# Running sums for the attention bias, copied 32 times into DRAM in the first phase and read back row by row

## The chip, the cores and the metric

The kernel runs on one core of a Trainium2 chip. The metric is the device time of one execution in microseconds (us). The core has a matrix engine (PE, with its weight loads PEld), three engines for elementwise work (DVE, ACT, POOL), and a queue for transfers on SP; ACT can issue transfers too. DMA means a transfer between the chip's memory (DRAM) and the on-chip memory of 128 partitions (SBUF). PE writes into eight banks.

## The reference, cut to what matters

```python
# q, k, v: [4 batches, 8 heads, 576 positions, 64], s: [4, 8, 576]
cum   = np.cumsum(np.maximum(s, 0.0), axis=-1)
bias  = -(cum[:, :, :, None] - cum[:, :, None, :])
scores = q @ k.T / 8 + np.minimum(bias, 0.0)      # causal: later keys at -1e9
attn  = softmax(scores)                            # normalised with + 1e-9
x = (attn @ v) as 2304 tokens of 512
x = ((x @ w_a) * (x @ w_b)) @ w_out                # inner width 1536
h = x @ w_in                                       # inner width 2048
out = (max(h, 0) + alpha * min(h, 0)) @ w_out2
```

Each of the 32 rows of running sums (batch and head) has 576 values. The bias of a query is the row minus the query's own value, so a tile of scores with 128 queries in its partitions needs the whole row in each of its partitions.

## The kernel before, in words

The 2304 tokens go through the two feed-forward layers in four blocks of 512, 512, 512 and 768. A batch has 576 positions: the first 512 queries of a batch (`u` = 0) and the last 64 (`u` = 1) are handled apart. `first_attention` (L887) computes the first 512 queries of batch 0 alone, ahead of everything. Then each block's feed-forward matmuls (`ffn`, L1248 to L1250 and L1886 to L1888) are mixed with the attention steps for the next block, which `attention(blk)` lists.

Each product is computed from values split into a high and a low part (`xh`, `xl`, `wh`, `wl`), three matmuls each. Weights come as 64-bit numbers (`raw`), are decoded by ACT (`top`, L1029) and DVE (`w`, L292), stored to DRAM as 32-bit numbers (`w_d`), and read from there by later blocks.

The running sums: `s` is loaded into `s_sb` (32 partitions), DVE clips and scales it (L385) and sums along it (L386) into `cum`. L387 writes the 32 rows to DRAM (`cum_d`). For batches 0 and 1 (`SUMS_PE` = 2) and `u` = 0 the bias is added on PE from `cums` and `rows` (L557), which are made from `cum` right afterwards (L390 to L404). All other tiles use `load_sums` (L518): it reads a row of `cum_d` into the 128 partitions of `cb`, and `biases` (L606 on DVE, L610 on ACT) subtracts the query's value `cumq`. For `u` = 0 and batches 2 and 3 a load serves one head: one DMA reads 512 values of one row 128 times (16 loads). For `u` = 1 it serves two heads with 64 queries each: two DMAs read 576 values of a row 64 times each (32 DMAs).

The program fixes the order on each engine. It is made by a planner (`Order`) that runs through estimated times: each operation has a cost, and engines take the operation that can start first. `dma` (L315) counts 480 ns on SP, then 700 ns, then a time by its bytes and a landing time, and a chain with several DMAs plans each behind the landing of the one before. Steps of attention are put between feed-forward matmuls when the planner sees their inputs ready (`possible`). Each engine and each queue works in its program order: an instruction that waits holds up those behind it.

In the first microseconds ACT copies 16 small pieces of the unit matrix (`one_of`, L372), then runs one `Exp` on one column (L890). SP issues the load of `s` (L891), loads of `kq` for the first heads, the store of `cum_d` (L387), and more loads of `kq` and `v`. Weights are requested at `i == FROM_WEIGHTS` (2) in the loop of `first_attention`, five loads of `raw` of 512 KB.

Of the kernel before, what the change touches and what calls it, by code (L numbers as in the profile page):

```python
# [9 lines left out]
F32 = mybir.dt.float32  # L10
# [11 lines left out]
P = 128  # L22
# [26 lines left out]
def f32(ap):  # L49
    return ap.bitcast(F32)  # L50
# [16 lines left out]


FASTER, BEFORE, BEHIND, EARLY = 1.06, 6, 4, 4


SEVEN, PLAIN_1, PLAIN_2 = 3, 3, 4
# [139 lines left out]
def attention_two_moe_kernel(  # L212
# [10 lines left out]
    nc = tc.nc  # L223
    B, S, _ = v.shape
    H = kq_a.shape[1]
# [6 lines left out]
    QA = 4 * P  # L232
    QB = S - QA
# [5 lines left out]
    dram = ctx.enter_context(tc.tile_pool(name="dram", bufs=1, space=DRAM))  # L239
# [6 lines left out]
    raw = inner.enter_context(tc.tile_pool(name="raw", bufs=1))  # L246
    work = inner.enter_context(tc.tile_pool(name="work", bufs=1))
# [67 lines left out]
    def dma(o, i):  # L315
        yield {"sp": 480}, 700
        nc.sync.dma_start(o, i)
        yield {"dma": prod(o.shape) / (180 if o.dtype == U16 else 90)}, run.landing
# [14 lines left out]
    ident = const.tile([P, P], F32, name="ident")  # L333
# [20 lines left out]


    BH = B * H
    cum = raw.tile([BH, S + QB], F32, name="cum", tag="pb")
    cum_d = dram.tile([BH, S], F32, name="cum_d")
    cumq = const.tile([P, NR, BH], F32, name="cumq")


# [3 lines left out]
    NE = SUMS_PE * H  # L365
# [18 lines left out]
    def running_sums(s_sb):  # L384
        nc.vector.tensor_scalar(s_sb, s_sb, 0.0, 8.0, op0=ALU.max, op1=ALU.mult)  # L385
        nc.vector.tensor_tensor_scan(cum[:, 0:S], s_sb, s_sb, 0.0, op0=ALU.add, op1=ALU.max)  # L386
        nc.sync.dma_start(cum_d, cum[:, 0:S])  # L387
        nc.vector.tensor_copy(cum[:, S:S + QB], cum[:, QA:S])
        for i in range(0, P, D):
            nc.scalar.activation(cums[i:i + NE], cum[0:NE, 0:QA], AF.Copy)  # L390
            if i == 0:
                nc.vector.tensor_tensor(
                    cums[BH:BH + NE], cum[0:NE, 0:QA], f32(cums[0:NE]), op=ALU.subtract
                )
            else:
                nc.vector.tensor_copy(cums[i + BH:i + BH + NE], f32(cums[BH:BH + NE]))
        bases = acc[3][:, 0:4 * NE].rearrange("p (r b) -> p r b", b=NE)
        for r in range(4):
            nc.tensor.matmul(
                bases[:, r, :], cum[:, r * P:r * P + 1].to_broadcast([BH, P]), ident[:BH, 0:NE],  # L400
                start=True, stop=True,
            )
        nc.vector.scalar_tensor_tensor(
            rows, bases, less[:, 0:1], one_of, op0=ALU.mult, op1=ALU.add  # L404
        )
        sums = acc[2][:, 0:NR * BH].rearrange("p (r b) -> p r b", b=BH)
        for r in range(NR):
            nc.tensor.transpose(sums[:, r, :], cum[:, r * P:(r + 1) * P], ident[:BH, :BH])
        nc.vector.tensor_scalar(cumq[:, 0:4, :], sums[:, 0:4, :], -1.0, None, op0=ALU.mult)
        for j in range(2):  # L410
            own = slice(j * QB, (j + 1) * QB)
            nc.vector.tensor_scalar(
                cumq[own, 4, 0:BH // 2], sums[own, 4, j:BH:2], -1.0, None, op0=ALU.mult
            )
# [22 lines left out]
    def slot():  # L437

        ring.append(ring.pop(0))
        if ring[-1] in reader:  # L440
            run.need(reader[ring[-1]])
        return ring[-1]
# [53 lines left out]
    def load_kq(b, hp, u):  # L496

        got = []

        def chain():  # L500
            if not u and b >= STACK:
                halves = [run.spawn(stack(b, 2 * hp + j, got), run.t) for j in range(2)]
                yield halves[0]
                yield halves[1]
                return
            yield of_kq
            kq = raw.tile([P, 2 * QA], F32, name="kq", tag="kq", bufs=KQ)
            got.append(kq)
            if u:
                yield from dma(kq[:, 0:S + P], kq_b[b, hp])  # L510
            else:
                for j in range(2):
                    own = slice(j * D, (j + 1) * D)
                    yield from dma(kq[own], kq_a[b, 2 * hp + j, own])

        kq_t[b, hp, u] = got, run.spawn(chain())

    def load_sums(b, h, u):  # L518

        got = []  # L520

        def chain():
            yield of_c1 if u else of_c0
            nk = S if u else QA
            cb = raw.tile([P, nk], F32, name=f"cb{u}", tag=f"cb{u}", bufs=2 if u else CB)
            got.append(cb)
            n = P // (u + 1)
            for j in range(u + 1):
                bh = b * H + (u + 1) * h + j
                yield from dma(  # L530
                    cb[j * n:(j + 1) * n], cum_d[bh:bh + 1, 0:nk].to_broadcast([n, nk])
                )

        cb_t[b, h, u] = got, run.spawn(chain())

    def q_k(b, hp, r, dst):

        got, ready = kq_t[b, hp, 0]
        run.need(ready)
        n = P * (r + 1)  # L540
        if b >= STACK:
            for d, (qs, kh, kl) in zip(dst, got):
                for i, k in enumerate((kh, kl)):
                    nc.tensor.matmul(  # L544
                        d, qs[:, r * P:n], k[:, 0:n], start=i == 0, stop=i == 1
                    )
            run.pe(4 * (n / 2.4 + 13))
            if r == 3:
                kq_t.pop((b, hp, 0))
                for s in (of_kl, of_w32, of_w32, of_stack) * 2:  # L550
                    run.give(s)
            return
        own = [slice(j * D, (j + 1) * D) for j in range(2)]
        if b < SUMS_PE:
            for j, o in enumerate(own):
                bh = b * H + 2 * hp + j
                nc.tensor.matmul(  # L557
                    dst[j], rows[o, r, bh:bh + 1].to_broadcast([D, P]), cums[o, 0:n], start=True,
                    stop=False,
                )  # L560
            run.pe(n / 2.4)
        for j, o in enumerate(own):
            nc.tensor.matmul(  # L563
                dst[j], got[0][o, QA + r * P:QA + n], got[0][o, 0:n], start=b >= SUMS_PE, stop=True
            )
        run.pe(4 * n / 2.4)
        if r == 3:
            kq_t.pop((b, hp, 0))
            run.give(of_kq)
# [63 lines left out]
    def both(b, hp, rs):  # L633
        for j in range(2):
            biases(b, 2 * hp + j, rs)
# [90 lines left out]
    def s23(b, hp, r):  # L726
        at = [slot(), slot()]
        dst = [banks[i][:, 0:P * (r + 1)] for i in at]
        q_k(b, hp, r, dst)
        for j, d in enumerate(dst):  # L730
            soften(b, 2 * hp + j, (r,), [d], at[j])
# [152 lines left out]

    HP = H // 2

    def first_attention():  # L887
        nonlocal ahead
        s_sb = work.tile([BH, S], F32, name="s_sb", tag="z4")
        nc.scalar.activation(alpha_sb[:, 0:1], ident[:, 0:1], AF.Exp)  # L890
        nc.sync.dma_start(s_sb, s)  # L891
        for i in range(2):
            load_kq(0, i, 0)
        run.now = 2000.0
        run.pump()
        running_sums(s_sb)
        run.now = 5000.0
        for rs in ((0, 1), (2,)):
            both(0, 0, rs)
        for i in range(HP + 2):  # L900
            if i + 2 < HP:
                load_kq(0, i + 2, 0)
            if i < HP:
                load_v(0, i, 0)
                both(0, i, (3,))
                s01(0, i)
                if i + 1 < HP:
                    both(0, i + 1, (0, 1))
            if 0 <= i - 2:
                av(0, i - 2, 0)  # L910
            if i < HP:
                s23(0, i, 2)
                if i + 1 < HP:
                    both(0, i + 1, (2,))
                s23(0, i, 3)
            if i == FROM_WEIGHTS:
                nc.sync.dma_start(alpha_sb, alpha)
                ahead = AHEAD
                prefetch()
            if i == FROM_LEAD:  # L920
                for f, args in plan[0][0]:
                    f(*args)
            if 0 <= i - 1 < HP:
                for c in range(3):
                    for j in range(2):
                        turn(0, 2 * (i - 1) + j, c)
            if i >= FROM_STEPS:
                for f, args in plan[0][1][:STEPS]:
                    f(*args)
                del plan[0][1][:STEPS]  # L930
# [978 lines left out]
    for blk in range(NB):  # L1909
# [11 lines left out]
        if 1 <= blk < NB - 1:  # L1921
            n = max(0, blk * S + QA - blocks[blk + 1][0])
# [72 lines left out]
```

## Time and profile before

| what | value |
|---|---|
| time of the runs, median (lowest to highest) | 985.03 us (984.52 to 985.04), 3 runs |
| span of the profiled execution, first to last instruction | 982.3 us |
| what lies around the span, against the median | 2.7 us |
| PE busy | 963.1 us (98%) |
| DVE, ACT, POOL busy | 748.5, 558.7, 223.7 us |
| moved by DMA | 196.78 MB, mean 200 GB/s |

The profiled execution has no time of its own besides its span, so the difference of 2.7 us is taken as what an execution needs before its first and after its last instruction. PE is busy nearly all the time, so what matters is the few microseconds in which it is not.

### The profile page before, as it was taken

The numbers are of one execution on the slowest core, as the hardware profiler recorded it, in microseconds if no ns is written. First come the engines' busy times: TensorE is split into PE (matmuls) and PEld (weight loads), VectorE is DVE, ScalarE is ACT, GpSimd is POOL, SyncE is SP. The second block draws the span as 40 slices with busy tenths as digits, with TensorE's granted clock in tenths as the row PEclk, the third lists the DMA queues.
The fourth block names the chain that finished last, engine by engine and source line by source line (L and its number), as shares of the span: only waits on it lengthen the run. The fifth ranks groups of instructions, "written<-read, shape, count | busy, mean of one in ns | idle before, by whom it ended". The sixth has DMA issues, their size and how long they took to land.

```text
span 982.3 us, 15862 instructions
## 1 busy us (share of the span) xinstructions
PE 963.1 (98%) x5235; PEld 810.3 (82%) x5235; DVE 748.5 (76%) x1743; ACT 558.7 (57%) x1173; POOL 223.7 (23%) x290
## 2 busy tenths in 40 slices
PE   6989999999999999999999999999999999999998
PEld 5557787778888878888888888888899999999997
DVE  7777886986878788888478868666497888787782
ACT  6856675775855555665455547544552333476453
POOL 2131110431124234563135434522100000000000
PEclk9999999999999999999999999999999999999999
DMA  7589999899788979688388785855402212112101
GB/s 181 185 262 320 347 332 322 293 323 329 245 271 259 304 245 312 194 257 293 112 270 260 218 264 194 251 172 183 165 22 94 78 66 87 43 47 82 61 5 65
DMA packets 140083, 196.78 MB, mean 200 GB/s; under 512 B 35744, under 2 KB 79776, under 8 KB 140000
## 3 DMA queue, kind: packets, MB, share of 16 engines
q1 hardware_dynamic: 130208, 177.93, 58.0%
q10 hardware_dynamic: 9792, 17.83, 4.9%
q8 instruction: 41, 0.67, 0.3%
q14 instruction: 42, 0.34, 0.1%
HBM read 152.13 MB, written 43.59 MB: 199 GB/s over the span
## 4 chain that ended last, share of the span: by engine, by line
PE 84%; DMA 8%; DVE 5%; issue 1%; ACT 1%; SPq 0%; POOL 0%; ACTq 0%; DVEq 0%
PE bank L1248 18%; PE bank L1249 18%; PE bank L1250 18%; PE bank L1886 5%; PE bank L1888 4%; PE bank L1887 4%; DMA cb<-cum_d 3%; PE bank L1735 2%; PE bank L1734 2%; PE bank L1736 2%; PE bank L801 2%; DMA raw<-in_w_dram 2%; PE bank L563 2%; PE bank L544 1%; PE bank L741 1%
## 5 line engine op out<-in xcount | busy, mean ns | idle before, releaser
L1248 PE MATMUL bank<-xh,wh 128*128 128x512 f32 (+1 forms) x620 | 237.9, 384 | 2.0 <-DVE g L292 2.0
L1250 PE MATMUL bank<-xh,wl 128*128 128x512 f32 (+1 forms) x620 | 234.0, 377 | 0.0
L1249 PE MATMUL bank<-xl,wh 128*128 128x512 f32 (+1 forms) x620 | 234.0, 377 | 0.0
L284 ACT ACTIVATE wh<-raw 128x512 fp32r<-128x512 f32 (+1 forms) x198 | 115.1, 592 | 84.4 <-PE bank L1249 35.0
L1248 PEld LDWEIGHTS bank<-xh,wh 128*128 128x128 f32 x620 | 116.4, 188 | 26.1 <-issue 4.6
L1250 PEld LDWEIGHTS bank<-xh,wl 128*128 128x128 f32 x620 | 116.4, 188 | 19.3
L1249 PEld LDWEIGHTS bank<-xl,wh 128*128 128x128 f32 x620 | 116.4, 188 | 18.6
L301 POOL TENSOR_TENSOR wl<-raw,wh 128x512 fp32r<-128x512 f32 x69 | 91.5, 1329 | 110.9 <-ACT wh L284 71.1
L301 DVE TENSOR_TENSOR wl<-raw,wh 128x512 fp32r<-128x512 f32 (+1 forms) x135 | 84.6, 640 | 33.7 <-ACT wh L284 27.8
L276 ACT ACTIVATE z<-z,mn 128x512 f32<-128x512 f32 (+4 forms) x144 | 82.8, 577 | 47.3 <-DVE mn L292 45.9
L1248 PE MATMUL bank<-gh,wh 128*128 128x512 f32 (+1 forms) x240 | 89.5, 373 | 0.0
L1249 PE MATMUL bank<-gl,wh 128*128 128x512 f32 (+1 forms) x240 | 88.7, 370 | 0.4 <-DVE gl L301 0.2
L1250 PE MATMUL bank<-gh,wl 128*128 128x512 f32 (+1 forms) x240 | 88.5, 369 | 0.0
L284 ACT ACTIVATE gh<-g 128x512 fp32r<-128x512 f32 x84 | 52.8, 629 | 43.5 <-DVE g L292 40.1
L1886 PE MATMUL bank<-wh,gh 128*128 128x512 f32 x192 | 76.4, 398 | 0.0
L1029 ACT ACTIVATE top<-raw 128x512 f16<-128x512 bf16 x90 | 68.5, 784 | 12.3 <-DMA raw<-in_w_dram 10.9
L1888 PE MATMUL bank<-wh,gl 128*128 128x512 f32 x192 | 74.8, 389 | 0.0
L1887 PE MATMUL bank<-wl,gh 128*128 128x512 f32 x192 | 74.8, 389 | 0.0
L301 DVE TENSOR_TENSOR gl<-g,gh 128x512 fp32r<-128x512 f32 x69 | 51.6, 748 | 18.8 <-ACT gh L284 18.0
L292 DVE STREAM_TRANSPOSE zt<-z 128x384 f32<-128x384 f32 (+2 forms) x88 | 55.7, 648 | 2.4 <-DMA zd<-zt 1.4
L616 POOL TENSOR_SCALAR_AFFINE_SELECT z<-z 64x64 f32<-64x64 f32 (+2 forms) x80 | 34.0, 432 | 97.3 <-DVE z L606 63.7
L311 DVE TENSOR_SCALAR z<-z,sm 128x512 f32<-128x512 f32 (+4 forms) x100 | 55.0, 573 | 1.3
(151 smaller groups left out, 1918.1 us busy)
## 6 DMA issues: line engine op xcount, KB each, us to landing
raw<-w_d SPq DMA_DIRECT2D x91, 512.0 KB, 4.3
raw<-in_w_dram SPq DMA_DIRECT2D x90, 512.0 KB, 5.6
w_d<-w ACTq DMA_DIRECT2D x46, 256.0 KB, 5.0
zd<-zt SPq DMA_DIRECT2D x48, 192.0 KB, 5.0
pt<-zd SPq DMA_DIRECT2D x48, 192.0 KB, 4.9
kq<-in_kq_a_dram SPq DMA_DIRECT2D x16, 512.0 KB, 5.7
vb<-in_v_dram SPq DMA_DIRECT2D x112, 64.0 KB, 4.4
zd<-zt SPq DMA_DIRECT2D x24, 256.0 KB, 4.0
```

The costliest lines, as they stand in the source:

```text
L276: nc.scalar.activation(o, i, func, **k)
L284: nc.scalar.activation(o, i, AF.Copy, scale=by)
L292: f(*args, **k)
L301: (nc.gpsimd if eng == "pool" else nc.vector).tensor_tensor(o, i0, i1, op=ALU.subtract)
L311: (nc.gpsimd if eng == "pool" else nc.vector).tensor_scalar(o, i, s0, s1, op0=ALU.mult, op1=ALU.mult)
L1029: nc.scalar.activation(top.bitcast(F16).rearrange("p (n t) -> p n t", t=2)[:, :, 1], r.bitcast(BF16)[:, 4:4 + 4 * WN].rearrange("p (n t) - ...
L1248: nc.tensor.matmul(o, wh, ih, start=first, stop=False)
L1249: nc.tensor.matmul(o, wh, il, start=False, stop=False)
L1250: nc.tensor.matmul(o, wl, ih, start=False, stop=last)
L1886: nc.tensor.matmul(acc[t], gh[:, c], wh, start=first, stop=False)
L1887: nc.tensor.matmul(acc[t], gh[:, c], wl, start=False, stop=False)
L1888: nc.tensor.matmul(acc[t], gl[:, c], wh, start=False, stop=last)
```

## The change

`s` is loaded four times, into the four quarters of 128 partitions, the first by SP and three by ACT. DVE then sums in 128 partitions. The store of `cum_d` behind the sums is gone. In its place `spread_sums`, called in the loop of `first_attention` at `i == 1`, issues four DMAs on SP, and each writes eight copies of each of the 32 rows, from its own quarter of `cum`. A load of `cb` then reads as many rows of the copies as it fills partitions, every fourth partition from 32 rows (`u` = 0, four DMAs) or every second from 64 rows (`u` = 1, two DMAs).

```diff
+ROWS = 32
...
-    cum = raw.tile([BH, S + QB], F32, name="cum", tag="pb")
-    cum_d = dram.tile([BH, S], F32, name="cum_d")
+    RM = P // BH
+    cum = raw.tile([P, S + QB], F32, name="cum", tag="pb")
+    cum_d = dram.tile([BH * ROWS, S], F32, name="cum_d")
...
     def running_sums(s_sb):
         nc.vector.tensor_scalar(s_sb, s_sb, 0.0, 8.0, op0=ALU.max, op1=ALU.mult)
         nc.vector.tensor_tensor_scan(cum[:, 0:S], s_sb, s_sb, 0.0, op0=ALU.add, op1=ALU.max)
-        nc.sync.dma_start(cum_d, cum[:, 0:S])
-        nc.vector.tensor_copy(cum[:, S:S + QB], cum[:, QA:S])
+        nc.vector.tensor_copy(cum[0:BH, S:S + QB], cum[0:BH, QA:S])
...
-            n = P // (u + 1)
-            for j in range(u + 1):
-                bh = b * H + (u + 1) * h + j
-                yield from dma(
-                    cb[j * n:(j + 1) * n], cum_d[bh:bh + 1, 0:nk].to_broadcast([n, nk])
-                )
+            bh = b * H + (u + 1) * h
+            n = ROWS * (u + 1)
+            for k in range(P // n):
+                yield from dma(cb[k::P // n], cum_d[bh * ROWS:bh * ROWS + n, 0:nk])
...
+    def spread_sums():
+        n = ROWS // RM
+        for i in range(RM):
+            nc.sync.dma_start(
+                cum_d.rearrange("(b c) n -> b c n", c=ROWS)[:, i * n:(i + 1) * n],
+                cum[i * BH:(i + 1) * BH, 0:S].unsqueeze(1).to_broadcast([BH, n, S]),
+            )
+
     def first_attention():
         nonlocal ahead
-        s_sb = work.tile([BH, S], F32, name="s_sb", tag="z4")
+        s_sb = work.tile([P, S], F32, name="s_sb", tag="z4")
+        for i in range(RM):
+            (nc.scalar if i else nc.sync).dma_start(s_sb[i * BH:(i + 1) * BH], s)
         nc.scalar.activation(alpha_sb[:, 0:1], ident[:, 0:1], AF.Exp)
-        nc.sync.dma_start(s_sb, s)
...
                 s23(0, i, 3)
+            if i == 1:
+                spread_sums()
             if i == FROM_WEIGHTS:
```

The readers of `cum` in the first phase (bases, transposes) take its first 32 partitions, as before.

## Rows read from the trace of the kernel before

**Rows 1.** The page, its head and busy time of the engines.
```profile
span 982.3 us, 15862 instructions
PE 963.1 (98%) x5235; PEld 810.3 (82%) x5235; DVE 748.5 (76%) x1743; ACT 558.7 (57%) x1173; POOL 223.7 (23%) x290
```

**Rows 2.** Busy time by stretch of the span, the first two stretches.
```profile
0.00:30.00 30.00, 21.26 (x119) 16.50 (x121) 20.17 (x96) 19.73 (x67) 6.89 (x20) 0.94 0.74 199
30.00:60.00 30.00, 26.48 (x165) 15.78 (x163) 23.80 (x92) 24.45 (x66) 4.55 (x10) 0.94 0.65 188
```

**Rows 3.** Waits of PE: us in total, times, longest.
```profile
PE bank L399 <- DVE cum L386: 5.4, 1, 5.4
PE bank L563 <- DMA kq<-in_kq_a_dram: 3.1, 2, 2.6
PE bank L1248 <- DVE g L292: 2.0, 1, 2.0
...
PE bank L544 <- DVE ovl L301: 0.8, 1, 0.8
...
PE bank L1249 <- DVE gl L301: 0.2, 1, 0.2
```

**Rows 4.** The chain that ended last, its pieces in time: start, length, what.
```profile
0.74 1.90 DMA s_sb<-in_s_dram
...
39.63 5.92 DMA kq<-in_kq_b_dram
45.57 7.42 DMA cb<-cum_d
```

**Rows 5.** Timeline of the first 24 us: start, length, engine, line.
```profile
0.74 0.40 SPq L891 DMA_DIRECT2D s_sb<-in_s_dram  x1
...
2.03 2.16 ACT L372 ACTIVATE one_of<-ident 32x16 f32<-32x16 f32 x16
...
2.54 0.98 POOL L1021 MEMSET top<- 128x512 int32 x2
2.67 1.17 DVE L385 TENSOR_SCALAR s_sb<-s_sb 32x576 f32<-32x576 f32 x1 [0.43 <-DMA s_sb<-in_s_dram]
...
4.21 0.20 ACT L890 ACTIVATE alpha_sb<-ident 128x1 f32<-128x1 f32 x1
5.24 0.32 SPq L387 DMA_DIRECT2D cum_d<-cum  x1
...
9.19 0.58 PE L563 MATMUL bank<-kq 64*128 64x128 f32 x1 [0.48 <-DMA kq<-in_kq_a_dram]
...
16.51 0.59 SPq L317 DMA_DIRECT2D vb<-in_v_dram  x1
```

**Rows 6.** All transfers onto ACT's queue from one line, first 80 us.
```profile
L1185 ACTq DMA_DIRECT2D w_d<-w x7: 326/326/358, 38.7 to 77.1; - x7
```

**Rows 7.** DMA issues: count, KB each, median us from issue to landing.
```profile
vb<-in_v_dram SPq DMA_DIRECT2D x112, 64.0 KB, 4.4
...
pb<-zd SPq DMA_DIRECT2D x16, 320.0 KB, 4.3
cb<-cum_d SPq DMA_DIRECT2D x32, 144.0 KB, 6.7
...
cb<-cum_d SPq DMA_DIRECT2D x16, 256.0 KB, 6.2
```

**Rows 8.** Timeline of DVE from 50 to 54 us.
```profile
53.08 0.52 DVE L606 TENSOR_SCALAR z<-cb,cumq 128x576 f32<-128x576 f32 x1 [4.71 <-DMA cb<-cum_d]
```

**Rows 9.** Busy time by stretch again; the last two columns are DMA share and GB/s.
```profile
8.00:10.00 2.00, 1.52 (x11) 1.23 (x10) 0.35 (x3) 0.00 (x0) 0.00 (x0) 1.00 1.01 226
...
22.00:28.00 6.00, 6.00 (x38) 4.34 (x38) 3.98 (x26) 4.31 (x13) 0.69 (x1) 0.72 1.02 399
...
30.00:38.00 8.00, 8.00 (x64) 5.05 (x60) 6.78 (x36) 7.76 (x24) 1.68 (x4) 1.00 0.00 0
```

**Rows 10.** The decoding of the weights by ACT in the first 80 us.
```profile
L1029 ACT ACTIVATE top<-raw x11: 766/788/854, 37.0 to 75.0; 128x512 f16<-128x512 bf16 x11
```

More of the change, by code (lines that the diff above doesn't have):

```diff
@@ L399, in running_sums @@
             nc.tensor.matmul(
-                bases[:, r, :], cum[:, r * P:r * P + 1].to_broadcast([BH, P]), ident[:BH, 0:NE],
+                bases[:, r, :], cum[0:BH, r * P:r * P + 1].to_broadcast([BH, P]), ident[:BH, 0:NE],
                 start=True, stop=True,
@@ L407, in running_sums @@
         for r in range(NR):
-            nc.tensor.transpose(sums[:, r, :], cum[:, r * P:(r + 1) * P], ident[:BH, :BH])
+            nc.tensor.transpose(sums[:, r, :], cum[0:BH, r * P:(r + 1) * P], ident[:BH, :BH])
         nc.vector.tensor_scalar(cumq[:, 0:4, :], sums[:, 0:4, :], -1.0, None, op0=ALU.mult)
```

## The prediction

> **What bounds the kernel now.** I read the page's head first: PE is busy 963.1 of 982.3 us [rows 1], so all other engines and transfers together can cost or give back only what they do to the 19.2 us in which PE is idle, plus any new idle time that they make. The busy time by stretch says where those microseconds lie: 30 less 21.26 and 26.48 leave 8.7 and 3.5 us idle before 60 us [rows 2]. The list of PE's waits gives causes. The largest is 5.4 us, once, for the running sums at the start; then 3.1 us in two waits for loads of `kq`, the longest 2.6; 2.0 us for `g`; the two that belong to later blocks, for `ovl` and `gl`, are 0.8 and 0.2 [rows 3]. So from the wait for `g`, at 70.6, to the last block PE waits 1.0 us in all: whatever the 48 loads of `cb` cost there, PE does not see it, and faster loads have next to nothing to give. The stretch before 71 us decides.
>
> The chain that ended last confirms it. It begins with the load of `s` at 0.74, goes through DVE, a load of `kq`, then PE and DVE alone up to a load of `kq` at 39.63 and one of `cb` at 45.57 that takes 7.42 us [rows 4], and from there through DVE to PE's wait for `g`. Behind that point PE is fed all the time, so a microsecond lost or won before it stays to the end.
>
> **The start: four loads of `s` in place of one.** Before, SP issues the load as its first transfer at 0.74, and it lands 1.90 us later; DVE starts L385 at 2.67 [rows 4, 5]. After, L385 works on all 128 partitions and so waits for all four loads, three of which stand in ACT's program. There they come behind the 16 copies of `one_of`, which run from 2.03 to 4.19, and ahead of the `Exp` that starts at 4.21 [rows 5]. ACT works in its program's order, so the first of the three is issued at about 4.2. An issue on ACT takes 0.33 us (326 ns median) [rows 6]; with a step of 0.35 the third is issued at 4.9, and the longest of the seven, 0.358, gives the same.
>
> How long the third load takes is not in the trace. From below, the same 72 KB took 1.90 us when hardly anything else was moving [rows 4]. From above, 64 KB of `v` take 4.4 us at the median beside full queues [rows 7]. At 5 us there will be traffic: SP is no longer held by L387, which waited for `cum` until 5.24 [rows 5], so several `kq` loads run at once. But nothing stands ahead of the three on ACT's queue, and the size is that of the 1.90 us row, so I take 2.6, nearer to the lower end. The load lands at 7.5 (6.8 to 9.3), and L385 starts 4.8 us later than before (4.1 to 6.6).
>
> Three things give some of this back. L385 took 1.17 us beside POOL's clearing of `top`, which ran from 2.54 to 3.52 [rows 5]; the same kind of operation, of the same width, took 0.52 us at 53.08 [rows 8]. At 7.5 us POOL is idle, so I count 0.65 us won (0 if POOL was not the reason). That L385 now has 128 partitions in place of 32 I cost at nothing: the 0.52 us row has 128 of them too. Second, the store L387 with its wait leaves SP's queue, so the `kq` loads that stand behind it go out earlier, and PE's wait of 0.48 us for them at 9.19 [rows 5] goes: minus 0.5. Their early arrival gives no more, since PE and DVE then need `rows` and `cums`, which need `cum`. The `Exp` behind the loads and everything behind it on ACT wait for `cum` anyway. So PE's first scores come 4.8 - 0.65 - 0.5 = 3.65 us later (4.1 - 0.65 - 0.5 = 2.95, to 6.6 - 0.5 = 6.1). From there to 39 us the chain holds engines alone, and the load at 39.63 [rows 4] is issued behind their work, so all shifts.
>
> **The spread.** Four DMAs write 32 x 32 x 576 x 4 bytes = 2.36 MB where 74 KB were written. They stand in SP's program near the `v` load at 16.51 [rows 5], ahead of the five weight loads. Two rates bound them: 399 GB/s, which the weights reached from 22 to 28 us, and 226 GB/s, of the stretch with `kq` loads of 64 partitions [rows 9]. That is 5.9 to 10.4 us; sources of 32 partitions are nearest to the 64, so I take 10.4. The Trainium skill, SBUF — State Buffer, section Door 1: The DMA port swizzle, says that 32 partitions reach only 8 of 16 ports, for at most some 218 GB/s, as 64 do. The `kq` rows' 226 GB/s agrees about; by the page the spread would be an estimated 10.8 us.
>
> What hides it: from 30 to 38 us nothing moves at all, 0 GB/s [rows 9], and the first weights are wanted by ACT at 37.0 [rows 10]. Issued 3.65 us late, at about 20, the spread ends at 30.5, the 2.6 MB of five weight loads at 399 GB/s would end at 37, the first of them at about 32, and ACT now wants it at 40.7. So it costs nothing, with over 8 us to spare for the first load. If the hole were not there, it would cost its 10.4 us on the weights.
>
> **The loads of `cb`.** For `u` = 1 they stay two DMAs of 144 KB. Before 71 us only these occur, so SP issues no more there than before. Their landing takes 6.7 us at the median, while 320 KB of `pb` need 4.3 [rows 7]. If reading one row 64 times were the whole of that, 2.4 us would be won on each; if it is only queueing behind weights, nothing. One of them counts: DVE waits 4.71 us for it at 53.08 [rows 8], and the chain goes on from there to PE's wait of 2.0 us for `g` [rows 3]. So the gain is 0 to 2.0. Since the load was issued in the midst of the fullest traffic, I take the lower part, 0.4.
>
> For `u` = 0 one DMA becomes four of 64 KB: 48 issues more, all for batches 2 and 3, whose scores are computed in blocks 1 and 2, where PE waits for nothing but the 1.0 us above. In the chain of a load the planner puts each behind the landing of the one before, so the bias is planned some 10 us later and the order of DVE, ACT and SP shifts a little. The loads are asked for a whole pair of heads ahead, and PE has feed-forward work between, so I count 0; as the bound above I take one new wait as long as PE's longest for a load, 2.6 us [rows 3].
>
> **Sum.** 3.65 - 0.4 = 3.25 us on a span of 982.3, which is 985.6; with the 2.7 us around it, 988.3. Against the median of the runs, 985.03, it is 0.33% more. A difference of 0.2%, 2.0 us, is about what can be told from no change here.
>
> **Rivals.**
> The `cb` loads pay (0.08). If landing really hangs on the 64 readings of one row, the load at 45.57 lands early enough that both PE waits behind it go: 2.6 for `kq`, behind the pair's first load, and 2.0 for `g` [rows 3]: 4.6 less against 3.65 more gives 984.1, no change that can be told. It decides from 1.7 us of gain upward. Against it: `cb` of 256 KB, with 128 readings of one row, lands in 6.2, sooner than the 144 KB with 64 [rows 7], the wrong way round for a price by readings.
>
> The loads on ACT do not wait for `one_of` (0.07): if ACT's queue issues them while the copies are still to run, at about 1.5 to 2.2, they land by 4.1 to 4.8; L385 is 1.4 to 2.1 late, and less 0.5 and 0.4 that makes 985.5 to 986.2. Against it: ACT's order, with `Exp` starting 0.02 us behind the last copy.
>
> The many small loads hurt later (0.14). Each of 16 loads needs four issues and landings; where the fourth holds up a bias and through it DVE, which works in order, PE gets a new wait: at the price of 2.6 us [rows 3], 988.3 + 2.6 = 990.9, and 993.5 if in both blocks. It decides once a bias comes later than the feed-forward work ahead of it lasts. The Trainium skill, DMA: Bandwidth & Descriptors, section Rules for kernel authors, speaks for this rival: join small transfers, since under 64 KB one mostly pays overhead. The trace has 64 KB of `v` at 4.4 us against 6.2 for 256 KB of `cb` [rows 7], which agrees; by the page's fixed cost of about 2 us each, three more in a row would make a load an estimated 6 us later.
>
> The spread is slow (0.04): below some 130 GB/s it takes over 18 us, the weights come after ACT wants them, and each further microsecond is lost: 990 to 994.
>
> **Numbers.** My forecast has 0.67, with its own range 986.0 (2.95 - 2.0 = 0.95 more than 985.03) to 991.1 (6.1 more). Over all cases I give 985.8, which takes in part of the second rival, to 992.0, which takes in the third at its single price. Faster by over 0.2% needs two gains at their ends: 0.04. Within 0.2%: the first two rivals and the lower edge of the forecast, 0.15. Slower: 0.81.
>
> **What would show it.** In the profile after, ACT's three loads of `s_sb` are issued from 4.2 to 5.3, L385 starts near 7.5 and takes about 0.5, PE's wait for `cum` grows from 5.4 to about 9.5, and the one at 9.19 for `kq` is gone. The stretch before 40 us is 3.65 us longer for the same work, with the transfers' hole filled. PE's waits behind 75 us stay at about 1 us. I am wrong if L385 starts before 5, if ACT waits for `raw` before 45 us, if the wait of DVE for `cb` at 53 goes and PE's with it, or if new PE waits appear in blocks 1 and 2.

## The result and the profile after

The median after is 991.21 us (989.64 to 991.54, 4 runs) against 985.03 us (984.52 to 986.05, 4 runs) before: ratio 1.0055, 95% interval 1.004 to 1.0071. So the change costs 6.2 us; forecast were 3.25, with 988.3 us and a range of 985.8 to 992.0. Direction and range held. The profiled execution took 989.64 us on a span of 987.9, 5.6 us more than [rows 1] where 3.25 were forecast. What lies around the span is thus 1.7 us, and 1.7 to 1.8 in every other run that has both times; the 2.7 taken ahead of the prediction set the span of one execution against the median of others. The forecast of 3.25 us more does not hang on it. Inside the sum two terms were off, in opposite directions: PE's first matmul is 9.48 us late and not 4.8 - 0.65 = 4.15, and 3.75 us of that are given back by its last one, where 0.5 + 0.4 = 0.9 were forecast.

The page of the kernel after, its head and the engines' busy time, the answer to [rows 1]:

```profile
span 987.9 us, 15955 instructions
PE 961.4 (97%) x5235; PEld 808.2 (82%) x5235; DVE 742.1 (75%) x1738; ACT 561.7 (57%) x1177; POOL 223.8 (23%) x291
```

PE does no more work than before; it is idle for 26.5 us in place of 19.2. The same kernel by stretch (length, then PE, PEld, DVE, ACT, POOL busy, granted clock, DMA share, GB/s), beside [rows 2]:

```profile
0.00:30.00 30.00, 11.86 (x66) 8.55 (x67) 14.05 (x65) 14.08 (x52) 4.82 (x15) 0.99 0.53 119
8.00:10.00 2.00, 0.00 (x0) 0.00 (x0) 0.00 (x0) 0.00 (x0) 0.00 (x0) 1.00 1.10 224
...
24.00:36.00 12.00, 8.70 (x54) 5.78 (x52) 10.12 (x65) 9.99 (x33) 3.11 (x6) 0.86 1.00 235
...
30.00:60.00 30.00, 27.16 (x186) 18.00 (x185) 22.37 (x97) 25.98 (x67) 5.40 (x11) 0.96 0.94 297
```

All of the loss is ahead of 30 us: 11.86 us busy there against 21.26, 9.4 less, and slightly more than before in the next stretch. From 8 to 10 us no engine computes while transfers run at 224 GB/s.

PE's waits in the kernel after (total, times, longest), beside [rows 3]:

```profile
PE bank L402 <- DVE cum L390: 14.8, 1, 14.8
...
PE bank L564 <- DMA kq<-in_kq_a_dram: 1.9, 1, 1.9
PE bank L1260 <- DVE g L295: 1.5, 1, 1.5
...
PE bank L1261 <- DVE gl L304: 0.2, 1, 0.2
```

One wait has grown by much, from 5.4 to 14.8. Apart from one of 1.7 us that is now 2.1 and a new one of 0.2, the others are shorter or the same, and the second wait for `kq` is gone. What the 14.8 consist of stands in the timeline of the first 16 us, to be read beside [rows 5]:

```profile
1.20 3.12 SPq L320 DMA_DIRECT2D kq<-in_kq_a_dram  x5
...
2.02 1.30 ACT L376 ACTIVATE one_of<-ident 32x16 f32<-32x16 f32 x9
...
3.14 0.42 ACTq L900 DMA_DIRECT2D s_sb<-in_s_dram  x1
3.23 0.95 ACT L376 ACTIVATE one_of<-ident 32x16 f32<-32x16 f32 x7
4.96 1.59 ACTq L900 DMA_DIRECT2D s_sb<-in_s_dram  x2
...
6.60 0.20 ACT L901 ACTIVATE alpha_sb<-ident 128x1 f32<-128x1 f32 x1 [2.42 <-DMA kq<-in_kq_a_dram]
12.84 0.46 DVE L389 TENSOR_SCALAR s_sb<-s_sb 128x576 f32<-128x576 f32 x1 [10.61 <-DMA s_sb<-in_s_dram]
```

ACT issues the first load of `s` at 3.14, ahead of the last seven `one_of` copies, the second at 4.96 and the third only after 6 us. The `Exp` behind them is listed as having waited 2.42 us for a load of `kq`, which it does not read. The chain that ended last begins in the same way (start, length, what):

```profile
1.82 4.39 DMA kq<-in_kq_a_dram
6.23 6.48 DMA s_sb<-in_s_dram
12.84 0.47 DVE s_sb L389
```

The third load of `s` goes out at 6.23, 0.02 us behind the landing of a `kq` load, and takes 6.48 us itself. The order list of the built program says why one waits for the other. Each transfer signals its landing on one of eight semaphores, taken in turn over SP's and ACT's transfers, and an issue that reuses one waits until its earlier user has landed. ACT's program reads:

```
L376 ACTIVATE one_of<-ident 32x16 x15
L900 DMA s_sb<-in_s_dram 32x576 [waits DMAHW0_49]
L900 DMA s_sb<-in_s_dram 32x576 [waits DMAHW1_49]
L900 DMA s_sb<-in_s_dram 32x576 [waits DMAHW2_49]
```

Number 0 is the load of `s` on SP, 1 and 2 are SP's first two `kq` loads, of 64 partitions and 256 KB each. The first of them lands at 4.94 and the second at 6.21, and ACT's second and third load go out 0.02 us behind each. Transfers by issue (count, KB each, median us to landing), beside [rows 7]:

```profile
cb<-cum_d SPq DMA_DIRECT2D x32, 144.0 KB, 5.1
...
cb<-cum_d SPq DMA_DIRECT2D x64, 64.0 KB, 4.1
cum_d<-cum SPq DMA_DIRECT2D x4, 576.0 KB, 9.0
...
s_sb<-in_s_dram ACTq DMA_DIRECT2D x3, 72.0 KB, 6.2
s_sb<-in_s_dram SPq DMA_DIRECT2D x1, 72.0 KB, 1.9
```

The same 72 KB take 1.9 us on SP, as the first transfer of all, and 6.2 at the median on ACT, beside `kq`. And the 144 KB loads of `cb` land in 5.1 where they took 6.7.

Where the rest is given back can be read from one piece of work that both kernels do in each block, 20 matmuls from `pb` and `vb`. First its rows of the kernel before, then of the kernel after (timeline of PE):

```profile
107.04 0.80 PE L862 MATMUL bank<-pb,vb 128*64 128x64 f32 x20
...
429.36 0.80 PE L862 MATMUL bank<-pb,vb 128*64 128x64 f32 x20
...
695.71 0.80 PE L862 MATMUL bank<-pb,vb 128*64 128x64 f32 x20
```

```profile
113.84 0.80 PE L863 MATMUL bank<-pb,vb 128*64 128x64 f32 x20
...
434.95 0.80 PE L863 MATMUL bank<-pb,vb 128*64 128x64 f32 x20
...
701.44 0.80 PE L863 MATMUL bank<-pb,vb 128*64 128x64 f32 x20
```

PE is 9.48 us late at its first matmul (14.84 against 5.36), 6.80 at 107 us, 5.59 at 429, and 5.73 at 696 and at its last matmul.

### The profile page after: what moved, and what is told of

Same layout as the page of the kernel before. It is cut to its first block, busy times and chain, and to the rows that moved or that the text cites. A ratio compares the mean times of both kernels' runs of the same rounds, so it can differ in the third digit from the quotient of the medians.

```text
span 987.9 us, 15955 instructions
## 1 busy us (share of the span) xinstructions
PE 961.4 (97%) x5235; PEld 808.2 (82%) x5235; DVE 742.1 (75%) x1738; ACT 561.7 (57%) x1177; POOL 223.8 (23%) x291
## 4 chain that ended last, share of the span: by engine, by line
PE 92%; DMA 5%; DVE 2%; ACT 0%; SPq 0%; issue 0%; DVEq 0%; ACTq 0%
PE bank L1260 21%; PE bank L1261 20%; PE bank L1262 20%; PE bank L1898 5%; PE bank L1900 4%; PE bank L1899 4%; PE bank L802 2%; PE bank L1747 2%; PE bank L1746 2%; PE bank L1748 2%; PE bank L545 2%; DMA kq<-in_kq_a_dram 2%; PE bank L564 2%; PE bank L742 1%; DMA raw<-in_w_dram 1%; PE bank L863 1%
## 5 line engine op out<-in xcount | busy, mean ns | idle before, releaser
L1041 ACT ACTIVATE top<-raw 128x512 f16<-128x512 bf16 x90 | 68.5, 785 | 10.4 <-DMA raw<-in_w_dram 9.1
L304 DVE TENSOR_TENSOR gl<-g,gh 128x512 fp32r<-128x512 f32 x70 | 53.7, 768 | 15.9 <-ACT gh L287 14.9
L279 ACT ACTIVATE m<-bank 128x512 f32<-128x512 f32 x48 | 28.5, 593 | 42.7 <-PE bank L1262 39.6
```

Source lines behind the costliest of these rows:

```text
L279: nc.scalar.activation(o, i, func, **k)
L304: (nc.gpsimd if eng == "pool" else nc.vector).tensor_tensor(o, i0, i1, op=ALU.subtract)
L1041: nc.scalar.activation(top.bitcast(F16).rearrange("p (n t) -> p n t", t=2)[:, :, 1], r.bitcast(BF16)[:, 4:4 + 4 * WN].rearrange("p (n t) - ...
```

## The experiments

The theory after the result was: the late start is the whole loss, and its cause is where the three loads of `s` stand and what they wait for; the rest of the change is worth some 3 us. The rivals: the late start is made good later anyway and something else costs; or the new `cb` loads cost in blocks 1 and 2; or the spread does. Runs beside each other on the same chip give the ratios; five rounds each, three where it is said.

**The start alone.** Four loads of `s` as after; one store of 72 KB in place of the copies, at `i == 1`, and `cb` read as before.

```diff
-    cum_d = dram.tile([BH * ROWS, S], F32, name="cum_d")
+    cum_d = dram.tile([BH, S], F32, name="cum_d")
...
+                yield from dma(
+                    cb[j * n:(j + 1) * n], cum_d[bh:bh + 1, 0:nk].to_broadcast([n, nk])
+                )
...
     def spread_sums():
...
+        nc.sync.dma_start(cum_d, cum[0:BH, 0:S])
```

> The four loads of s stay as in the changed kernel, three of them on ACT; the copies are gone: 32 rows are written to DRAM once, at the place of the spread, and cb is read as before the change. Theory 1 (the late start carries the whole loss): DVE begins to clip s at 12.8 us as in the changed kernel, and the time is 990 to 993. Theory 2 (the spread and the 48 more loads cost about half): 986 to 989.

Measured: 992.93 us (991.53 to 993.87, 6 runs), ratio 1.0079 (1.0065 to 1.0093). PE's wait for `cum` is 14.9 as after. The late start is there without any copies, and the kernel is no faster than after. So the copies and the loads from them are not what costs; by the medians they give 1.7 us back and by the ratios 2.4, though the two intervals overlap.

**One load.** All of the change except the four loads: `s` goes once into 32 partitions, and one DMA of 2304 KB spreads it.

```diff
-    RM = P // BH
-    cum = raw.tile([P, S + QB], F32, name="cum", tag="pb")
+    RM = 1
+    cum = raw.tile([BH, S + QB], F32, name="cum", tag="pb")
...
-        s_sb = work.tile([P, S], F32, name="s_sb", tag="z4")
+        s_sb = work.tile([BH, S], F32, name="s_sb", tag="z4")
```

> The copies stay; s is loaded once by SP into 32 partitions, and one transfer spreads the sums from there. Theory 1: DVE begins to clip s at 2.7 us, PE's wait for the sums is 5.4 again, its wait for kq at 9 us is gone, and the time is 982.5 to 985. Theory 2: 986 to 989, with new PE waits behind 75 us or a late decoding of the weights (behind 42 us).

Measured: 981.94 us (979.49 to 985.08, 12 runs), ratio 0.9974 (0.9959 to 0.9988). PE's wait for `cum` is 5.4 again. From the chain that ended last (start, length, what):

```profile
2.69 1.16 DVE s_sb L389
...
5.37 1.86 PE bank L402 x8
```

Without the late start the rest of the change makes the kernel faster than before, by 0.26%.

**All four loads on SP**, ahead of `kq`.

```diff
-            (nc.scalar if i else nc.sync).dma_start(s_sb[i * BH:(i + 1) * BH], s)
+            nc.sync.dma_start(s_sb[i * BH:(i + 1) * BH], s)
```

> The changed kernel with all four loads of s on SP, ahead of kq. Theory 1 with the cause that ACT's loads wait for semaphores of earlier kq loads and then stand beside them: clipping begins at 4 to 4.5, the time is 983.5 to 986. If four loads in place of one are slow wherever they are issued: clipping at 7 or later, 987 or more.

Measured: 982.49 us (980.65 to 987.46, 12 runs), ratio 0.9976 (0.996 to 0.9992); PE's wait for `cum` is 6.2, each of the four loads lands in 1.9 us, and DVE starts on `s_sb` at 4.16 (chain):

```profile
4.16 0.47 DVE s_sb L389
```

Four loads on 128 partitions are not what costs either; it is where three of them are issued.

**ACT's loads first**, ahead of `one_of`. The loads move up in the program and nothing else does.

```diff
     mask = raw.tile([P, QA], F32, name="mask", tag="kl", bufs=KL)
+    s_sb = work.tile([P, S], F32, name="s_sb", tag="z4")
+    for i in range(RM):
+        (nc.scalar if i else nc.sync).dma_start(s_sb[i * BH:(i + 1) * BH], s)
```

> The changed kernel with the three ACT loads of s issued ahead of the copies of the unit matrix, so they are ACT's first instructions. If their place behind the kq loads is the cause (in the order of the semaphores and of the transfers): clipping begins at 4 to 5, the time is 984 to 986.5. If ACT's queue itself is slow beside a busy SP queue: clipping at 8 or later, 988 or more.

Measured: 983.62 us (982.07 to 986.57, 12 runs), ratio 0.9985 (0.9974 to 0.9997). In the built program these three loads wait for no semaphore, being the first users. Timeline of this kernel's first 13 us:

```profile
0.73 1.37 ACTq L376 DMA_DIRECT2D s_sb<-in_s_dram  x3
...
5.62 0.46 DVE L392 TENSOR_SCALAR s_sb<-s_sb 128x576 f32<-128x576 f32 x1 [3.39 <-DMA s_sb<-in_s_dram]
```

They go out by 2.1, and the last still takes 3.83 us (chain of waits) where each of the four on SP took 1.9. So about 4.6 us of the third load's lateness are its later issue (6.23 against 1.66) and 2.65 its longer flight (6.48 against 3.83). These three kernels came out up to 1 us faster than expected, and this one starts on `s_sb` later than the 4 to 5 us expected.

**Two loads**, one on SP and one on ACT, 64 partitions, in the position of the change.

```diff
-    RM = P // BH
-    cum = raw.tile([P, S + QB], F32, name="cum", tag="pb")
+    RM = 2
+    cum = raw.tile([RM * BH, S + QB], F32, name="cum", tag="pb")
...
-        s_sb = work.tile([P, S], F32, name="s_sb", tag="z4")
+        s_sb = work.tile([RM * BH, S], F32, name="s_sb", tag="z4")
```

> The changed kernel with two loads of s, one on SP and one on ACT, into 64 partitions, and a spread in two transfers. The one load on ACT stands behind the copies of the unit matrix but waits for no semaphore of a kq load. If the semaphores of the second and third load are the larger part of the late start: clipping begins at 7 to 7.5 in place of 12.8 us, the time is 985 to 987.5. If the place in ACT's program or the traffic beside it is: clipping at 10 or later, 988 or more.

Measured: 985.48 us (983.26 to 989.85, 12 runs), ratio 1.0015 (1.0001 to 1.0028). Timeline of the first 13 us:

```profile
3.14 0.42 ACTq L900 DMA_DIRECT2D s_sb<-in_s_dram  x1
...
8.00 0.45 DVE L389 TENSOR_SCALAR s_sb<-s_sb 64x576 f32<-64x576 f32 x1 [5.77 <-DMA s_sb<-in_s_dram]
```

The one ACT load waits for the semaphore of SP's load of `s` alone, goes out at 3.14 as the first of three did, and takes 4.84 us (chain) with nothing ahead of it on ACT's queue. DVE starts half a microsecond later than expected. So the further 4.84 us of the kernel after (12.84 against 8.00) come from its second and third loads, which are held for `kq` and then fly beside more of it.

The kernels that hold the copies now stand in a row by the time at which DVE starts on `s_sb`: 2.69 us (one load) 981.94; 4.16 (all on SP) 982.49; 5.62 (ACT's first) 983.62; 8.00 (two loads) 985.48; 12.84 (after) 991.21. PE's first matmul follows at 5.37, about 6.2, 7.6, 10.0 and 14.84, so 9.5 us later at PE cost 9.3 us at the end by the medians, and 8.0 us by the ratios (1.0055 less 0.9974 of 985).

**The store later.** The kernel before with only its store of `cum_d` moved from its place behind the sums to `i == 1`.

```diff
-        nc.sync.dma_start(cum_d, cum[:, 0:S])
...
+            if i == 1:
+                nc.sync.dma_start(cum_d, cum[:, 0:S])
```

> The kernel before, with one edit: the store of the 32 rows of sums is issued where the changed kernel issues its spread, so SP's kq loads no longer stand behind a wait for the sums. No copies, one load of s, cb read as before. If the gain of the one-load kernel is only the freed queue: 981.5 to 982.5, as that one. If the copies have a part in it: PE's first scores are 1.4 us earlier as there, but the time is 983 to 985.

Measured: 983.84 us (981.58 to 986.05, 12 runs), ratio 0.999 (0.9976 to 1.0003), not told from no change. The trace shows an effect all the same. PE's timeline, first of the kernel before, then of this one:

```profile
9.20 0.58 PE L557 MATMUL bank<-cums,rows 64*128 64x256 f32 x1
...
9.64 0.56 PE L557 MATMUL bank<-cums,rows 64*128 64x256 f32 x1
...
14.27 0.73 PE L563 MATMUL bank<-kq 64*128 64x128 f32 x2
...
19.49 0.89 PE L768 MATMUL bank<-ident,z 128*128 128x128 f32 x3 [1.72 <-POOL z L311]
```

```profile
8.37 0.56 PE L556 MATMUL bank<-cums,rows 64*128 64x256 f32 x2
...
12.76 0.44 PE L562 MATMUL bank<-kq 64*128 64x128 f32 x4
...
17.78 0.90 PE L767 MATMUL bank<-ident,z 128*128 128x128 f32 x3 [2.12 <-POOL z L311]
```

Both start at 5.36 or 5.37, but the first transposes come at 17.78 instead of 19.49, 1.71 us sooner, though the wait of 0.48 for `kq` was all the idle time there was. Most of the rest is in how the matmuls of two heads, from 64 partitions each, run beside each other. Here both halves of `kq` are there and the two start together: two of 64x256 take 0.56 at 8.37. Before, the second half comes late (the wait at 9.19 [rows 5]), the two heads fall out of step, and the same two matmuls start 0.44 apart, at 9.20 and 9.64, each as long as the two here. The second pair of heads begins on `kq` at 12.76 instead of 14.27, so 1.51 of the 1.71 are made by then. The matmuls also get shorter on the way, the same 64x256 from 0.56 to 0.36, earlier here than before. The granted clock is 1.00 in these stretches of both, the higher level, so that column does not tell why; the runs do not settle it.

**Last queries alone.** The one-load kernel, with `u` = 0 read as before: one DMA, one row 128 times. Only the 32 loads of `u` = 1 use the copies.

```diff
+            if not u:
+                yield from dma(cb, cum_d[bh * ROWS:bh * ROWS + 1, 0:nk].to_broadcast([P, nk]))
+                return
```

> The one-load kernel with the copies used for the last 64 queries alone; the 16 loads for the first 512 queries read one row 128 times in one transfer, as before the change. If four small loads cost what one large one does, or their waits are covered: within 1 us of the one-load kernel, 981 to 983. If the 48 more issues hurt: 979 to 981. If the copies win in those loads: 983 to 984.5.

Measured: 979.84 us (979.09 to 983.54, 9 runs), ratio 0.9963 (0.995 to 0.9975), the lowest median of the study; by ratio two of the next kernels are level with it (0.996 and 0.9962). Against the store later (0.999) it has the copies and the new `u` = 1 loads, and is 0.27% or 2.7 us faster. The time is what was expected if the 48 further issues hurt, but the intervals of this kernel and of one load (0.9974) overlap, and the next run does not bear it out.

**Late start, last queries.** The kernel after with the same edit, so 48 transfers fewer.

> The changed kernel, late start and all, but the first 512 queries read one row 128 times in one transfer as before the change. If the 48 more transfers cost 2 us: 988.5 to 989.7 against 991.2. If they cost nothing that PE sees: 990.5 to 992. Clipping begins at 12.8 us.

Measured: 991.25 us (989.22 to 994.51, 6 runs), ratio 1.0053 (1.0032 to 1.0073), against 1.0055 for the kernel after. The 48 further transfers cost nothing that can be measured.

**All on SP, last queries**: that edit on the kernel with all four loads on SP.

> Four loads of s on SP ahead of kq, the copies used for the last 64 queries alone, the first 512 as before the change. If the two gains add up: 979 to 981. If the four small loads are no worse than one of 128 readings: as the kernel with all loads on SP, 982 to 983. Clipping begins at 4.2 us either way.

Measured: 981.67 us (980.23 to 983.61, 9 runs), ratio 0.996 (0.9945 to 0.9976). It cannot be told from the two kernels that it is made of.

**One row, strided.** The one-load kernel, where the four DMAs of `u` = 0 keep their every fourth partition but read one row 32 times each.

```diff
+                if u:
+                    src = cum_d[bh * ROWS:bh * ROWS + n, 0:nk]
+                else:
+                    src = cum_d[bh * ROWS:bh * ROWS + 1, 0:nk].to_broadcast([n, nk])
+                yield from dma(cb[k::P // n], src)
```

> The one-load kernel with the four small transfers for the first 512 queries kept, every fourth partition each, but all reading one row 32 times. If reading one row many times is slow: the 64 transfers of 64 KB land at a median of 5 us or more in place of 4.3, and kq_b of 352 KB at 6.3 to 7 in place of 5.6. If one row is as good as 32: 4.1 to 4.5 and about 5.6. Time 981 to 984.

Measured (3 rounds): 982.07 us (979.56 to 984.84, 10 runs), ratio 0.9962 (0.9945 to 0.9979). The 64 KB loads land in 4.0 us from one row, and in 4.3 from 32 copies (one load). So reading one row 32 times is not slower.

**Halves.** The last-queries kernel, where each DMA of `u` = 1 reads 32 copies twice each and fills 64 partitions in a row, as before, in place of every second.

```diff
+            for j in range(2):
+                rows_j = cum_d[(bh + j) * ROWS:(bh + j + 1) * ROWS, 0:nk]
+                yield from dma(
+                    cb[j * D:(j + 1) * D], rows_j.unsqueeze(1).to_broadcast([ROWS, 2, nk])
+                )
```

> One load of s; for the last 64 queries each transfer fills 64 partitions in a row, from 32 copies read twice each; the first 512 queries read one row 128 times. Told by the landing of the 32 transfers of 144 KB: if the copies are what makes them land sooner (6.7 before, 6.0 with copies beside the one-row loads), it stays at about 6.0; if it is that every second partition is filled, it goes back to 6.5 to 6.9. Time 980 to 983.5.

Measured (3 rounds): 984.92 us (982.66 to 985.89, 10 runs), ratio 0.9988 (0.9974 to 1.0002). The transfers by issue, first of last queries alone, then of halves:

```profile
kq<-in_kq_b_dram SPq DMA_DIRECT2D x16, 352.0 KB, 6.3
...
cb<-cum_d SPq DMA_DIRECT2D x32, 144.0 KB, 6.0
```

```profile
kq<-in_kq_b_dram SPq DMA_DIRECT2D x16, 352.0 KB, 7.3
...
cb<-cum_d SPq DMA_DIRECT2D x32, 144.0 KB, 7.0
```

With copies as source and 64 partitions in a row as target, the load is as slow as before (6.7), and the `kq` load issued ahead of it slows with it. What made the loads of the change land sooner is the partitions that each fills, not that it reads copies. Part of it comes from the `u` = 0 loads: where these too are four that fill every fourth partition, the 144 KB land in 5.0 (one load, and one row, strided) and not 6.0. The time of halves is 1.4 us over the range that was expected either way.

**The spread twice.** The one-load kernel with `spread_sums()` called twice in a row; the second writes the same copies again.

```diff
                 spread_sums()
+                spread_sums()
```

> The one-load kernel with the spread written twice, 4.7 MB in place of 2.4, ahead of the weights. If the spread lies in the hole of the transfers with a few us to spare: the first decoding of weights waits for them, 3 to 7 us are lost, 985 to 989. If the hole has room for both: 981 to 983. If already the single spread is on the path: about 11 us more, 993.

Measured (3 rounds): 993.93 us (992.69 to 994.62, 4 runs), ratio 1.0093 (1.0079 to 1.0108), 12.0 us more than with one spread, as was expected if already the single spread is on the path. Timeline of SP, of PE and of ACT in this kernel:

```profile
14.54 15.12 SPq L891 DMA_DIRECT2D cum_d<-cum  x2
29.70 0.67 SPq L320 DMA_DIRECT2D kq<-in_kq_a_dram  x1
```

```profile
44.32 0.58 PE L564 MATMUL bank<-kq 64*128 64x128 f32 x1 [12.48 <-DMA kq<-in_kq_a_dram]
```

```profile
47.95 0.76 ACT L1042 ACTIVATE top<-raw 128x512 f16<-128x512 bf16 x1
```

What is late is not the weights, for which ACT has no wait listed, but the last head pair's `kq`, issued behind the spreads on SP. But the run does more than double the bytes. The second spread writes what the first one writes, so in the built program its issue waits for the first one's landing; it goes out at 29.08 and holds SP until then. So this `kq` load goes out at 29.70, where it goes at 15.25 with one spread, and then takes 14.6 us beside the second. How much of the 12.0 us is the held queue and how much the traffic, the run does not tell, nor whether the hole would hold two spreads issued together. How little room a single one leaves can be read from the kernels with one: the same `kq` load lands at 31.28 in one load, where PE begins with it at 31.41, and at 40.09 in the kernel after, where PE begins with it at 41.01.

## Why the prediction was right, and where it was not

**The verdict.** The kernel is slower, because the sums start late and PE has nothing before them: right, and shown by taking the late start away (one load, all on SP: both faster than before) and by keeping it alone (the start alone: no faster than after). That the range held is in part luck. The 991.21 lie 0.1 above the forecast's own range, which ended at 991.1; the 992.0 came from the price of the small loads, and these cost nothing. And the miss of 5.3 us at PE's first matmul was half made up by 2.85 us more that were given back than forecast.

**When ACT issues.** The step was that ACT works in its program's order, so the loads wait for `one_of` and go out from 4.2 to 4.9. That failed in both directions. The first went out at 3.14, before seven of the copies, as the rival of loads that do not wait for `one_of` said, though later than its 1.5 to 2.2. But the second and third went out at 4.96 and 6.23, held by the landings of `kq` loads through semaphores in common, a wait that neither the forecast nor that rival had. In the trace of before no transfer stood in such a place, but the list of a program's waits would have shown it.

**How long the load takes.** The term was 2.6 us, between 1.9 and 4.4; the third load took 6.48, over the upper bound. The argument was that nothing stood ahead of it on ACT's queue. Two loads has one ACT load alone, and that still takes 4.84: `kq` on SP's queue delays it. Issue and landing together: 6.23 + 6.48 = 12.7 where 7.5 was forecast. These two make the 5.4 us by which the start of L385 (now L389) was missed, 10.17 late instead of 4.8; 1.3 us of them are the issue (6.23 for 4.9) and 3.9 the flight (6.48 for 2.6). The Trainium skill, DMA: Bandwidth & Descriptors, section Issuing engines are not separate DMA queues, says that transfers from different engines end up on the same 16 DMA engines and interleave; the 4.84 and 6.48 agree, and the upper bound of 4.4 should not have been left for the lower end.

**What gives some of it back at once.** L389 beside an idle POOL takes 0.46 us for 1.17, so 0.71 for the 0.65 forecast: right in size. That POOL was the reason is not shown, since every run with the short time also has more than 32 partitions. The wait for `kq` at 9.19 is gone, as forecast, but that was worth 1.3 and not 0.5: the term took the wait alone, and left out that the two heads fall out of step behind it. From the first matmul to the first transposes were 19.49 - 5.36 = 14.13 us before. PE's timeline of the kernel after has those transposes here:

```profile
27.63 0.89 PE L769 MATMUL bank<-ident,z 128*128 128x128 f32 x3 [2.11 <-POOL z L314]
```

That is 27.63 - 14.84 = 12.79, or 1.34 less. The store later has 1.71 less with nothing else changed, so the move of the store does it.

**The spread.** Hidden, as forecast, but with far less room. Its four DMAs go out from 23.99 to 25.5 and land 5.4 to 12.8 us later, 9.0 at the median, so the last at 38.2: 14.2 us for the whole, where 10.4 were taken from the row of 64 partitions at 226 GB/s. The stretch from 24 to 36 us has 235 GB/s, but other loads are in it. The Trainium skill, SBUF — State Buffer, section Door 1: The DMA port swizzle, has at most some 218 GB/s for 32 partitions. In one load, where one DMA reads everything from the first 32 partitions, 203 GB/s move from 20 to 28 us, which agrees; the 235 come from four quarters in both halves, and do not contradict it. SP's and then ACT's timeline of the kernel after:

```profile
23.99 3.98 SPq L891 DMA_DIRECT2D cum_d<-cum  x4
...
35.39 3.52 SPq L320 DMA_DIRECT2D raw<-in_w_dram  x5
```

```profile
45.00 0.79 ACT L1041 ACTIVATE top<-raw 128x512 f16<-128x512 bf16 x1
```

The weights go out behind the spread, at 35.39, and ACT's first `top` comes at 45.0, 8.0 us later than at 37.0 [rows 10], with no wait listed. PE too is 8.0 us late there (its first matmul from the last `kq` at 41.01 for 33.05), so the spread adds nothing. But the first weights land at 43.31, 1.7 us before ACT takes them, where over 8 were forecast, and the last `kq` 0.9 us before PE does. So what the prediction named as next to be late, the weights, is not what is nearest: that is the last `kq`, as in the spread written twice.

**The loads of `cb`.** The term was 0.4 of a possible 2.0. The 144 KB land in 5.1 for 6.7 and DVE's wait goes from 4.71 [rows 8] to 3.50:

```profile
59.83 0.52 DVE L607 TENSOR_SCALAR z<-cb,cumq 128x576 f32<-128x576 f32 x1 [3.50 <-DMA cb<-cum_d]
```

Their worth was mis-sized: 1.7 us by the medians between the start alone and after, 2.7 between the store later and last queries alone. The rival that these loads pay held that a gain from 1.7 us up would cancel the slowdown; the gain was about that, but against a start that cost over twice the forecast it did not decide. Nor was its reason right, the 64 readings of one row: halves and one row, strided, show that the target's partitions make the difference. The Trainium skill, SBUF — State Buffer, section Door 1: The DMA port swizzle, has a ground for that: the first 64 partitions reach 8 of 16 ports, as do the last 64, and every second of 128 reaches all. The runs agree so far as 64 in a row land in 7.0 us and every second partition in 6.0; they do not show the ports.

**The small loads.** Costed at nothing, with a rival at 2.6: nothing, by late start, last queries (1.0053 against 1.0055). The Trainium skill's rule in DMA: Bandwidth & Descriptors, section Rules for kernel authors, to join transfers under 64 KB, spoke for the rival; its cost does not show in this kernel's time, since PE waits for none of these loads.

**The sum by what was measured.** PE's first matmul is 9.48 us late (forecast 4.8 - 0.65), less 1.34 by the first transposes (0.5), which leaves 8.14. What the `cb` loads give shows against the start alone, whose piece at 429 us comes here:

```profile
436.84 0.80 PE L865 MATMUL bank<-pb,vb 128*64 128x64 f32 x20
```

That is 1.89 later than after (434.95). 0.28 of it is there at 48.5 us, before any `cb` is used, so some 1.6 are the loads' (forecast 0.4), which leaves 6.5; PE's last matmul is 5.73 late. The remaining 0.8 are not the copies' either, for the start alone has them too: 8.35 late at the first transposes, 7.48 at 429. There PE's wait for `g` is 0.7 where it was 2.0 [rows 3]; why, stays open, since the waits for `kq` and `g` in the first 80 us differ by 1 to 2 us between kernels whose programs are alike there.

**A better kernel.** Last queries alone, 979.84 us, ratio 0.9963 (0.995 to 0.9975), beats both. One load, all on SP (with either form of `u` = 0), ACT's loads first and one row, strided, also beat the kernel before, and their intervals overlap with that one, so none of them can be named the best.

## What to carry to other kernels

A transfer's issue time follows from the semaphores that it waits for as much as from its place in the engine's program: where two queues draw on one set, look up in the built program whose landing the issue waits for before its place is taken as its time. A small load that starts the whole computation goes first on a queue, ahead of the bulk and not beside it on another. And of a change in several parts, price the parts apart: here parts that gave 0.3% came with one that cost 0.8%.

## What the runs showed of the hardware that was not expected

- 72 KB took 1.9 us as the first transfer. On ACT's queue, beside `kq` loads on SP's, they took 3.83 when issued at 1.66 (ACT's loads first), 4.84 at 3.14 (two loads) and 6.48 at 6.23 (the kernel after, 224 GB/s from 8 to 10 us). A queue of its own did not shield a small load from another queue's bulk.
- ACT issued a transfer at 3.14 while seven copies that stand ahead of it in its program were still to run, 3.23 to 4.18.
- Filling every second partition from 64 rows landed 144 KB in 6.0 us, filling 64 in a row took 7.0, and a 352 KB load issued next to it went from 6.3 to 7.3.
- 32 readings of one row in DRAM were no slower than 32 copies: 4.0 us against 4.3 for 64 KB.
- Two matmuls of 64x256 from 64 partitions each ran together in 0.56 us (8.37 in the store later). Behind a wait of 0.48 us of one of the two heads, they started 0.44 us apart and took 0.56 and 0.58 each. The same 64x256 later took 0.36, with the granted clock at 1.00 both times.
